# A recurrent-scan and gated-unit kernel: weight halves on two DMA queues, powers on GpSimd, and a narrower load of one matrix

## The chip, the cores and the metric

The kernel runs on one core of a Trainium2 chip (trn2). The metric is device time in microseconds (us), and I quote the median of the runs. A run whose time lies more than 1.5% above the fastest run of the same kernel is marked slow and is left out of ratios. Each profile is of a single run. Engine names are those of the profile: PE is the matmul engine TensorE, PEld its weight loads, DVE is VectorE, ACT is ScalarE, POOL is GpSimd, and SP is SyncE, which here only issues DMA transfers. A "q" after an engine's name means its instruction sequencer.

## The reference

Two branches read the same layer-normalised x (2048 tokens of 448 features). Branch A is a diagonal complex recurrence over the tokens, branch B a gated unit with 1792 hidden features.

```python
xn = layernorm(x)                                   # 2048 x 448
# A: recurrence of 448 complex states
dt      = exp(log_dt)
Lam_bar = exp(dt * (Lambda_re + 1j * Lambda_im))
Bu      = xn @ (((Lam_bar - 1) / Lam)[:, None] * (B_re + 1j * B_im)).T
h[t]    = Lam_bar * h[t-1] + Bu[t]
s       = 2 * real(h @ (C_re + 1j * C_im).T) + xn * Dskip
# B: gated unit
g       = silu((sigmoid(xn @ w_gate) * (xn @ w_up)) @ w_down)
out     = x + s * g
```

## The kernel before

The tokens are handled in four chunks of 512. For each chunk PE does the gate and up products (into `gu`, from where ScalarE and DVE take them out again into `hF`; this I call an eviction), the B product (xn with B_re and B_im, transposed to `bT`), the down product and the output product. DVE runs the scan (a hardware scan along the tokens) and the rotations around it. Once chunk 0 has reached the scan, PE and DVE are both full until near the end, so what can be gained lies in the head, before that point.

The order of the instructions on each engine is not the order of the text. A list scheduler inside the kernel (the planner, below) gives each operation an assumed cost, and sorts. `add("SP", 1.2, ...)` puts an operation that is assumed to take 1.2 us on SyncE. `chain=True` keeps the order of the text for DMA issues on one engine. A change of an assumed cost or of a transfer can reorder other engines too.

These are the parts that the change touches.

```python
def tload(keys, o, i, nbytes, r=(), chain=True):     # a transposing DMA, issued by SyncE
    add("SP", 1.2, lambda: Q.dma_start_transpose(out=o, in_=i), r=r, w=keys,
        dma=nbytes * 1.5, chain=chain)

# loads in the head: two queues, SyncE ("SP") and ScalarE ("ACT")
BLK = {"g": [(0, 2), (2, 4), (4, 7)], "u": [(0, 3), (3, 7)]}   # column blocks of w_gate, w_up
for t in range(4):
    load_x(t, 1, ("SP", "ACT")[t % 2])
load_w("SP", "g", 0, 0)                              # half 0: partitions 0-63
load_w("ACT", "g", 1, 0)                             # half 1: partitions 64-127
# ... parameters, then the other w_gate blocks ...
load("SP", "dbc", ...)                               # skip vector
load_x(4, 4)
for b in (0, 1):
    load_w("SP", "u", 0, b)                          # both halves of w_up on SyncE
    load_w("SP", "u", 1, b)

def columns():                                       # per-state parameters
    # ... PE turns three rows into columns, pv holds them ...
    add("ACT", 1.3, lambda: A.preload_act_table_set("exp_and_others"), ...)
    add("ACT", 0.2, lambda: A.activation(dt_b[:], pv[:, 0, :], ACT.Exp), ...)
    # ... four small DVE operations ...
    add("ACT", 0.2, lambda: A.activation(r_col[:], arg[:], ACT.Exp), ...)

def b_load():                                        # B, 448 x 448, to its transpose
    for i, m in enumerate((A_B_re, A_B_im)):
        tload([("bT", i)],  bT[:, 0:3, i, :], m[:, 0:384],   D * 768)
        tload([("bT3", i)], bT[:, 3:4, i, :], m[:, 320:448], D * 256)   # 128 columns
    # the last 64 states sit on partitions 64-127; copy them to 0-63 as well
    add("DVE", 0.53, lambda: V.tensor_copy(out=bT[0:H, 3, :, :], in_=bT[H:P, 3, :, :]), ...)
    for i in range(2):
        add("POOL", 0.9, lambda i=i: G.tensor_copy(out=bT6[:, :, i*H:i*H+H],
                                                   in_=bT[:, :, i, 384:448]), ...)

# issued by SyncE after b_load: eight transposes of chunk 1's xn (xnT), then w_down
```

448 is 3 x 128 + 64. Before the change the last transpose of each matrix takes 128 columns (320 to 447), of which 64 overlap the ones that were already loaded.

## Time and profile before

The median is 196.21 us (195.19 to 196.59) in three runs. The profiled run has a span of 195.0 us.

| before | us |
|---|---|
| first gate matmul | 9.15 |
| PE gaps, start to start: ScalarE's evictions late | 20.08 to 22.11 |
| PE gaps: DVE late (behind its wait for B_im) | 29.47 to 31.53 |
| PE gaps: DVE late | 34.57 to 35.74 |
| first B matmul | 34.55 |
| first scan on DVE | 40.66 |
| first gate matmul of chunk 1 | 42.77 |
| last PE instruction starts | 189.90 |

The page cuts the span into 40 slices of 4.9 us. Each digit is a busy share in tenths; PEclk is the clock that was granted to TensorE, the DMA row the mean busy share of the 16 DMA engines, and the GB/s row what they moved. The last line counts packets by size.

```profile
PE   7799696899999999999989999999999999999990
DVE  3736978999999999999999999999999999992074
PEclk9999999999999999999999999999999999999999
DMA  5899994399700014300004410000001000101002
GB/s 139 203 211 220 159 161 90 79 316 182 210 0 3 0 27 87 78 0 0 0 5 104 98 37 24 0 24 3 24 0 47 3 0 0 52 25 47 0 27 67
DMA packets 30166, 13.41 MB, mean 69 GB/s; under 512 B 19651, under 2 KB 30150, under 8 KB 30150
```

From the ninth slice on PE and DVE read 9 almost throughout, until near the end. The holes in PE (the two 6s and the 8 between them and the run of 9s) are all in the first eight slices.

The windows view gives the busy time of each engine in a stretch, in this order: stretch, its length, then PE, PEld, DVE, ACT and POOL with the number of instructions, then PEclk, DMA share and GB/s.

```profile
20.00:40.00 20.00, 15.71 (x127) 7.47 (x123) 17.86 (x38) 14.51 (x23) 10.50 (x32) 1.00 0.78 120
40.00:165.00 125.00, 122.75 (x899) 56.98 (x904) 124.69 (x205) 59.26 (x78) 16.61 (x28) 1.00 0.20 48
```

Between 20 and 40 us PE is busy 15.71 us of 20. Between 40 and 165 us DVE is busy 124.69 us of 125 and PE 122.75. Nothing can be gained there by feeding them sooner.

The waits view says which engine and line waited for what: us in total, times, longest.

```profile
DVE xd L427 <- DMA dbc<-in_A_Dskip_dram: 2.6, 1, 2.6
ACT c_r L512 <- DVE c_arg L504: 2.2, 1, 2.2
PE gu L653 <- DVE hF L670: 1.7, 1, 1.7
PE gu L653 <- ACT hF L667: 1.7, 1, 1.7
DVE bT L598 <- DMA bT<-in_A_B_im_dram: 1.6, 1, 1.6
```

The 20 us hole is a chain: DVE waited for the skip vector, so the argument `c_arg` came late, ScalarE stood at its second exponential (`c_r`), then loaded a table for 1.28 us, and the evictions `hF` that PE needed came after that. The hole at 29.5 us begins with DVE waiting for B_im before it could copy the half.

SyncE's own timeline (start, us, what it issued and how many) shows when the transposes went out:

```profile
13.06 1.36 SPq L328 DMA_DIRECT2D wU<-in_B_w_up_dram  x1
14.47 8.87 SPq L346 DMA_TRANSPOSE bT<-in_A_B_re_dram  x2
23.38 2.74 SPq L346 DMA_TRANSPOSE bT<-in_A_B_im_dram  x2
26.34 11.26 SPq L346 DMA_TRANSPOSE xnT<-xn  x8
37.65 0.59 SPq L328 DMA_DIRECT2D wd<-in_B_w_down_dram  x1
```

### The profile page before, as it was taken

What the parts mean: (1) busy time and instruction counts of PE and PEld (TensorE: products, weight loads), DVE (VectorE), ACT (ScalarE), POOL (GpSimd) and SP (SyncE); (2) the same over time, 40 slices, a digit from 0 to 9 for tenths busy, and PEclk for the clock granted to TensorE, in tenths of its full rate; (3) what the DMA queues carried; (4) which work ended last, traced back from release to release, by engine and by line L of the source; (5) the groups of instructions that cost most, each with busy time, mean ns of one, the idle gap of its engine ahead of it and who ended that gap; (6) DMA issues with size and microseconds to landing.
All of it is one profiled execution on the core that took longest, in us unless ns stands there. A gap on an engine that the chain in (4) does not pass through costs nothing.

```text
span 195.0 us, 3448 instructions
## 1 busy us (share of the span) xinstructions
PE 181.0 (93%) x1334; PEld 87.8 (45%) x1341; DVE 170.6 (87%) x313; ACT 85.7 (44%) x120; POOL 31.4 (16%) x85
## 2 busy tenths in 40 slices
PE   7799696899999999999989999999999999999990
PEld 2475353344445444444435444444435444455560
DVE  3736978999999999999999999999999999992074
ACT  2525996274877735324566341253336161211110
POOL 3220847100000770000257100000000000000000
PEclk9999999999999999999999999999999999999999
DMA  5899994399700014300004410000001000101002
GB/s 139 203 211 220 159 161 90 79 316 182 210 0 3 0 27 87 78 0 0 0 5 104 98 37 24 0 24 3 24 0 47 3 0 0 52 25 47 0 27 67
DMA packets 30166, 13.41 MB, mean 69 GB/s; under 512 B 19651, under 2 KB 30150, under 8 KB 30150
## 3 DMA queue, kind: packets, MB, share of 16 engines
q1 hardware_dynamic: 28930, 12.51, 29.9%
q10 hardware_dynamic: 1220, 0.69, 1.4%
q8 instruction: 10, 0.16, 0.4%
q14 instruction: 6, 0.05, 0.1%
HBM read 6.77 MB, written 1.84 MB: 44 GB/s over the span
## 4 chain that ended last, share of the span: by engine, by line
DVE 55%; PE 21%; SPq 9%; issue 7%; DMA 5%; ACT 1%; DVEq 0%
DVE hF L670 12%; DVE wv L759 9%; PE gu L653 5%; PE gu L820 5%; SPq L346 5%; PE acc L845 4%; PE acc L820 4%; SPq L328 4%; DVE ta L752 3%; DVE z L755 3%; DVE tb L753 3%; DVE o_t L851 3%; DVE tb L774 3%; DMA wG<-in_B_w_gate_dram 3%; DMA bT<-in_A_B_im_dram 2%
## 5 line engine op out<-in xcount | busy, mean ns | idle before, releaser
L653 PE MATMUL gu<-xnT,wG 64*128 64x512 bf16 (+1 forms) x217 | 47.0, 359 | 2.2 <-ACT hF L667 1.7
L653 PE MATMUL gu<-xnT,wU 64*128 64x512 bf16 x196 | 46.2, 376 | 1.7 <-DVE hF L670 1.7
L654 PE MATMUL gu<-xnT,wG 64*128 64x512 bf16 (+1 forms) x217 | 47.0, 359 | 0.0
L654 PE MATMUL gu<-xnT,wU 64*128 64x512 bf16 x196 | 46.2, 376 | 0.0
L667 ACT ACTIVATE sig<-gu 128x1024 f32<-128x1024 f32 x21 | 21.5, 1023 | 36.5 <-PE gu L654 36.3
L820 PE MATMUL acc<-wd,hF 128*128 128x448 bf16 x168 | 33.8, 353 | 0.0
L820 PEld LDWEIGHTS <-hF 128*128 128x128 bf16 x224 | 21.5, 98 | 21.3 <-issue 2.1
L653 PEld LDWEIGHTS <-wG 64*128 64x128 bf16 x217 | 20.1, 95 | 22.3 <-issue 2.7
L653 PEld LDWEIGHTS <-wU 64*128 64x128 bf16 x196 | 18.0, 94 | 22.9 <-issue 2.1
L670 DVE SCALAR_TENSOR_TENSOR hF<-sig,gu 128x1024 bf16<-128x1024 f32 x21 | 25.3, 1207 | 0.0
L759 DVE TENSOR_TENSOR_SCAN wv<-c_r,st,z 128x512 bf16<-128x512 f32 x18 | 23.0, 1277 | 0.0
L845 PE MATMUL acc<-cT,hT 128*128 128x448 bf16 x105 | 21.8, 353 | 0.0
L654 PEld LDWEIGHTS <-wG 64*128 64x128 bf16 x217 | 19.9, 95 | 2.5 <-issue 2.5
L654 PEld LDWEIGHTS <-wU 64*128 64x128 bf16 x196 | 17.9, 94 | 2.1 <-issue 2.0
L716 ACT CAST bus<-gu 128x1024 bf16<-128x1024 f32 x12 | 12.0, 1010 | 14.7 <-PE gu L705 14.7
L851 DVE TENSOR_TENSOR o_t<-acc,xd 128x448 bf16<-128x448 f32 x15 | 9.2, 613 | 9.2 <-PE acc L845 9.2
L705 PE MATMUL gu<-xnT,bT 128*128 128x512 bf16 x65 | 15.3, 379 | 1.1 <-issue 1.1
L845 PEld LDWEIGHTS <-hT 128*128 128x128 bf16 x119 | 11.5, 98 | 10.1 <-issue 0.4
L826 ACT ACTIVATE g_t<-acc 128x448 bf16<-128x448 f32 x12 | 6.4, 537 | 18.3 <-PE acc L820 18.3
L403 POOL TENSOR_SCALAR veb<-mv 128x2 bf16<-128x2 bf16 x6 | 2.7, 449 | 56.4 <-DVE mv L390 56.2
L389 DVE BATCH_NORM_STATS2 bst<-x_all 128x6 f32<-128x448 bf16 x16 | 9.4, 614 | 2.5 <-DMA x_all<-in_A_x_dram 2.5
L820 PE MATMUL gu<-wd,hF 128*128 128x448 bf16 x56 | 10.8, 352 | 0.0
(128 smaller groups left out, 242.2 us busy)
## 6 DMA issues: line engine op xcount, KB each, us to landing
out_dram<-o_t SPq DMA_DIRECT2D x15, 112.0 KB, 1.7
wd<-in_B_w_down_dram SPq DMA_DIRECT2D x1, 1568.0 KB, 7.1
x_all<-in_A_x_dram SPq DMA_DIRECT2D x3, 448.0 KB, 4.3
wU<-in_B_w_up_dram SPq DMA_DIRECT2D x2, 448.0 KB, 11.1
wG<-in_B_w_gate_dram SPq DMA_DIRECT2D x2, 336.0 KB, 4.5
wU<-in_B_w_up_dram SPq DMA_DIRECT2D x2, 336.0 KB, 9.8
wG<-in_B_w_gate_dram SPq DMA_DIRECT2D x2, 224.0 KB, 5.3
wG<-in_B_w_gate_dram ACTq DMA_DIRECT2D x2, 224.0 KB, 5.0
```

Source lines behind the costliest of these rows:

```text
L346: add("SP", 1.2, lambda: Q.dma_start_transpose(out=o, in_=i), r=r, w=keys, dma=nbytes * 1.5, chain=chain)
L389: add("DVE", 0.53, lambda: V.bn_stats(out=bst[b][:], in_=x_all[:, t, :]), r=[("x", t)], w=[("bst", b)])
L653: T.matmul(gu[a][:, 0, ts], lhsT=w_[0:H, s, ms], rhs=x[0:H, s, ts], start=(s == 0), stop=(s == 6))
L654: T.matmul(gu[a][:, 1, ts], lhsT=w_[H:P, (s + 1) % 7, ms], rhs=x[H:P, s, ts], start=(s == 0), stop=(s == 6))
L667: add("ACT", act(1024), lambda: A.activation(th, gu[a][:], ACT.Tanh, scale=0.5), r=[("gu", a)], w=[tk])
L670: add("DVE", dve1(1024), lambda: V.scalar_tensor_tensor(out=ho, in0=th, scalar=1.0, in1=gu[a][:], op0=ALU.add, op1=ALU.mult), r=[("gu", a) ...
L705: T.matmul(gu[a][:, i, :], lhsT=bT[:, kt, i, pt * P:pt * P + P], rhs=x[:, 2 * kt, :], start=False, stop=(kt == 2))
L716: add("ACT", act(1024), lambda u=u, a=a: A.copy(out=bus[u][:], in_=gu[a][:]), r=[("gu", a)], w=[("bus", u)])
L759: dve(1.194, lambda k=k: V.tensor_tensor_scan(out=wv[:, k, :], data0=rb, data1=z[:, k, :], initial=(st[pt][:, k, :] if c else 0.0), op0=AL ...
L820: T.matmul(d, lhsT=hF[c % 2][:, m, h, js], rhs=wd[:, ft, :], start=(ft == 0), stop=(ft == FT - 1))
L845: T.matmul(y, lhsT=hT[c % 2][:, hm, js], rhs=cT[:, cm, c0:c1], start=(i == 0), stop=(i == 6))
L851: add("DVE", dve1(n), lambda od=od, y=y, c0=c0, c1=c1: V.tensor_tensor(out=od, in0=y, in1=xq[:, c0:c1], op=ALU.add), r=[key, ("xd", q)], w ...
```

## The change

The intent is a shorter head. The two halves of each weight matrix arrive side by side on two queues, in fewer and larger blocks. The exponentials of the parameters become powers of e on GpSimd, which saves ScalarE a table load and takes small operations from DVE. Parameters and x tiles 4 to 7 are issued by GpSimd. The first transposes on PE lose a helper copy, tile 1's eviction is split between ScalarE and DVE, and w_down is issued before chunk 1's transposes. For B_re the last transpose takes just the 64 columns that are needed, straight to partitions 0 to 63, so that DVE's half copy can go. The scheduler's model of DMA times changes as well.

```diff
-    BLK = {"g": [(0, 2), (2, 4), (4, 7)], "u": [(0, 3), (3, 7)]}
+    BLK = {"g": [(0, 2), (2, 7)], "u": [(0, 7)]}
 ...
+    for k in range(3):
+        load_p("POOL", k)
     load_w("SP", "g", 0, 0)
     load_w("ACT", "g", 1, 0)
+    load_w("ACT", "g", 1, 1)
+    load_w("ACT", "u", 1, 0)
     load_w("SP", "g", 0, 1)
+    load_w("SP", "u", 0, 0)
     load("SP", "dbc", ...)
-    (both halves of w_up, and x tiles 4-7, on SyncE)
 ... columns():
-        add("ACT", 1.3, lambda: A.preload_act_table_set("exp_and_others"), ...)
-        add("ACT", 0.2, lambda: A.activation(dt_b[:], pv[:, 0, :], ACT.Exp), ...)
+        small(tt(dt_b[:], eb, pv[:, 0, :], ALU.pow), ["pv", "expc"], ["dt"])    # GpSimd
 ...
-        add("ACT", 0.2, lambda: A.activation(r_col[:], arg[:], ACT.Exp), ...)
+        small(tt(r_col[:], eb, arg[:], ALU.pow), ["arg", "expc"], ["r"])        # GpSimd
 ... b_load():
             tload([("bT", i)], bT[:, 0:3, i, :], m[:, 0:384], D * 768)
-            tload([("bT3", i)], bT[:, 3:4, i, :], m[:, 320:448], D * 256)
-        add("DVE", 0.53, lambda: V.tensor_copy(out=bT[0:H, 3, :, :], in_=bT[H:P, 3, :, :]), ...)
+            if i:
+                tload([("bT3", i)], bT[:, 3:4, i, :], m[:, 320:448], D * 256)
+            else:
+                tload([("bT3", i)], bT[0:H, 3:4, i, :], m[:, 384:448], D * 128)
 ... (the bT6 copies on GpSimd are split to match)
+    load_x(4, 4, "POOL", r=[("w", "g", 1, 6)])
     b_load()
+    load("SP", "wd", ...)                                   # moved ahead of chunk 1
 ... (warm-up matmuls, the wrap copy of xn and its transpose, the scheduler's DMA model: cut)
```

More of the change, by code (lines that the diff above doesn't have):

```diff
@@ L69 @@
 class Op:
-    __slots__ = ("idx", "eng", "cost", "fn", "pre", "suc", "late", "start", "end", "dma", "lat", "name", "left")
+    __slots__ = ("idx", "eng", "cost", "fn", "pre", "suc", "late", "start", "end", "dma", "lat", "name", "left", "rate")
 class Plan:
@@ L80, in __init__, with add @@
         self.last_of = {}
-    def add(self, eng, cost, fn, r=(), w=(), dma=0, lat=None, chain=False, name=""):
+    def add(self, eng, cost, fn, r=(), w=(), dma=0, lat=None, chain=False, name="", rate=230e3):
         o = Op()
@@ L85, in add @@
         o.lat = LAT.get(eng, 0.0) if lat is None else lat
-        o.pre, o.suc = {}, []
+        o.pre, o.suc, o.rate = {}, [], rate
         o.start = o.end = None
@@ L189, in solve @@
         dma_free = {}
+        landed = []
         while todo:
@@ L205, in solve @@
                 if e == "POOL":
-                    o.lat = 8.0
+                    o.lat = 6.0
                 else:
-                    q = dma_free[0] = max(dma_free.get(0, 0.0), o.end + 1.0) + o.dma / 280e3
-                    o.lat = q + 0.6 - o.end
+                    k = len(landed)
+                    if k >= 8:
+                        o.end = free[e] = max(o.end, landed[k - 8] + o.cost)
+                    q = dma_free[e] = max(dma_free.get(e, 0.0), o.end + 1.2) + o.dma / o.rate
+                    o.lat = q + 0.8 - o.end
+                    landed.append(q + 0.6)
             todo -= 1
@@ L302 @@
     veb = sbt("veb", [NT, 1])
-    halfc, negc = sbt("halfc", [1], FP32), sbt("negc", [1], FP32)
+    halfc, negc, expc = (sbt(n, [1], FP32) for n in ("halfc", "negc", "expc"))
     sdb = sbt("sdb", [NT, 1])
@@ L323, with load @@
     tag = lambda *k: k
-    def load(eng, key, nbytes, o, i, cost=0.45, r=()):
+    def load(eng, key, nbytes, o, i, cost=0.45, r=(), rate=230e3):
         e = {"SP": Q, "ACT": A, "POOL": G}[eng]
-        add(eng, 0.12 if eng == "ACT" else cost, lambda: e.dma_start(out=o, in_=i), w=[key] if not isinstance(key, list) else key,
-            r=r, dma=nbytes, chain=True)
+        add(eng, cost, lambda: e.dma_start(out=o, in_=i), w=[key] if not isinstance(key, list) else key,
+            r=r, dma=nbytes, chain=True, rate=rate)
     def load_x(t0, n, q="SP", r=()):
@@ L342, in load_w @@
              wgt[k][ps, :, m0 * P:m1 * P],
-             wsrc[k][:, c0 + m0 * P:c0 + m1 * P].rearrange("(s p) f -> p s f", p=H), r=r)
+             wsrc[k][:, c0 + m0 * P:c0 + m1 * P].rearrange("(s p) f -> p s f", p=H), cost=0.65, r=r, rate=145e3)
     def tload(keys, o, i, nbytes, r=(), chain=True):
@@ L354 @@
     add("POOL", 0.1, lambda: G.memset(negc[:], -1.0), r=["consts"], w=["consts"])
+    add("POOL", 0.1, lambda: G.memset(expc[:], math.e), w=["expc"])
     add("POOL", 0.1, lambda: G.memset(epsc[:], EPS), w=["epsc"])
@@ L362, with load_p @@
     add("ACT", 0.05, lambda: A.preload_act_table_set("sqrt_and_others"), w=["sqrttab"], lat=1.5, chain=True)
-    for t in range(4):
-        load_x(t, 1, ("SP", "ACT")[t % 2])
+    def load_p(eng, k):
+        load(eng, ("vrow", k), D * 2, vrow[k:k + 1, :], (A_log_dt, A_Lambda_im, A_Lambda_re)[k].unsqueeze(0), cost=0.25)
+    load_x(0, 1, "SP")
+    load_x(1, 1, "ACT")
+    load_x(2, 1, "SP")
+    load_x(3, 1, "ACT")
+    for k in range(3):
+        load_p("POOL", k)
     load_w("SP", "g", 0, 0)
     load_w("ACT", "g", 1, 0)
-    for k, vec in enumerate((A_log_dt, A_Lambda_im, A_Lambda_re)):
-        load("ACT" if k < 2 else "SP", ("vrow", k), D * 2, vrow[k:k + 1, :], vec.unsqueeze(0), cost=0.25)
+    load_w("ACT", "g", 1, 1)
+    load_w("ACT", "u", 1, 0)
     load_w("SP", "g", 0, 1)
-    load_w("ACT", "g", 1, 1)
-    for h in range(2):
-        load_w("SP", "g", h, 2)
+    load_w("SP", "u", 0, 0)
     load("SP", "dbc", P * D * 2, dbc[:], A_Dskip.unsqueeze(0).to_broadcast((P, D)))
-    load_x(4, 4)
-    for b in (0, 1):
-        load_w("SP", "u", 0, b)
-        load_w("SP", "u", 1, b)
     def warm_mm(n):
@@ L383, in f @@
                 T.matmul(gu[2][:, 0, :], lhsT=warm[:, 0:P], rhs=warm[:], start=True, stop=True)
-        add("PE", (0.43 if n > 1 else 0.22) * n, f, r=["warm"], w=[("gu", 2)])
+        add("PE", (0.38 if n > 2 else 0.22) * n, f, r=["warm"], w=[("gu", 2)])
     def stats(t):
@@ L415, in norm @@
                 r=[("x", t), ("mf", t), ("rs", t)], w=[("xn", b)])
-            add("POOL", 0.19, lambda: G.tensor_copy(out=xn[b][:, 448:512], in_=xn[b][:, 0:64]),
-                r=[("xn", b)], w=[("xnw", b)])
         else:
@@ L442, in pe_transpose, with f @@
         tp = flat(acc[a][:].bitcast(BF16)[:, 0:7 * P], 7, P)
-        def f(s0, s1):
-            for s in range(s0, s1):
+        def f():
+            for s in range(6):
                 T.transpose(tp[:, s, :], xn[b][:, s * H:s * H + P], ident[:, :])
-        add("PE", 0.36, lambda: f(0, 6), r=[("xn", b), "ident"], w=[("acc", a)])
-        add("PE", 0.06, lambda: f(6, 7), r=[("xnw", b), ("xn", b), "ident", ("acc", a)], w=[("acc", a)])
-        if t == 0:
-            add("ACT", 0.476, lambda: A.copy(out=xnT[0][:, 0:4, js], in_=tp[:, 0:4, :]),
+            T.transpose(tp[0:H, 6, :], xn[b][:, 384:448], ident[:, :])
+            T.transpose(tp[H:P, 6, :], xn[b][:, 0:H], ident[:, :])
+        add("PE", 0.46, f, r=[("xn", b), "ident"], w=[("acc", a)])
+        if t < 2:
+            add("ACT", 0.5, lambda: A.copy(out=xnT[0][:, 0:4, js], in_=tp[:, 0:4, :]),
                 r=[("acc", a)], w=[("xnT", 0, t, "a")])
@@ L453, in pe_transpose @@
                 r=[("acc", a)], w=[("xnT", 0, t, "b")])
-        elif t > 1:
+        else:
             add("DVE", 0.53, lambda: V.tensor_copy(out=xnT[0][:, :, js], in_=tp[:, :, :]),
-                r=[("acc", a)], w=[("xnT", 0, t, "a"), ("xnT", 0, t, "b")])
-        else:
-            add("ACT", 0.9, lambda: A.copy(out=xnT[0][:, :, js], in_=tp[:, :, :]),
                 r=[("acc", a)], w=[("xnT", 0, t, "a"), ("xnT", 0, t, "b")])
@@ L494, in columns @@
         pv = sbt("pv", [3, 4], FP32)
+        dt_b = C("dt", 4, BF16)
         add("DVE", 0.1, lambda: V.tensor_copy(out=pv[:].rearrange("p k i -> p i k"), in_=vps[:]), r=[("acc", a)], w=["pv"])
         dt_b = C("dt", 4, BF16)
-        add("ACT", 1.3, lambda: A.preload_act_table_set("exp_and_others"), r=[("sd", t) for t in range(4)], w=["exptab"])
-        add("ACT", 0.2, lambda: A.activation(dt_b[:], pv[:, 0, :], ACT.Exp), r=["pv", "exptab"], w=["dt"])
         lim, lre = pv[:, 1, :], pv[:, 2, :]
         K.update(lre=lre, lim=lim)
+        eb = expc[:].to_broadcast((P, 4))
         def small(fn, r, w):
-            add("DVE", 0.1, fn, r=r, w=w)
-        tt = lambda o, x, y, op: (lambda: V.tensor_tensor(out=o, in0=x, in1=y, op=op))
+            add("POOL", 0.4, fn, r=r, w=w)
+        tt = lambda o, x, y, op: (lambda: G.tensor_tensor(out=o, in0=x, in1=y, op=op))
         theta, arg, turn, r_col = C("theta"), C("arg"), C("turn"), C("r")
+        small(tt(dt_b[:], eb, pv[:, 0, :], ALU.pow), ["pv", "expc"], ["dt"])
         small(tt(theta[:], dt_b[:], lim, ALU.mult), ["dt", "pv"], ["theta"])
-        small(lambda: V.tensor_single_scalar(out=turn[:], in_=theta[:], scalar=1.0 / TWO_PI, op=ALU.mult),
+        small(lambda: G.tensor_single_scalar(out=turn[:], in_=theta[:], scalar=1.0 / TWO_PI, op=ALU.mult),
              ["theta"], ["turn"])
-        small(lambda: V.tensor_single_scalar(out=turn[H:P, 3:4], in_=theta[H:P, 3:4], scalar=-1.0 / TWO_PI,
+        small(lambda: G.tensor_single_scalar(out=turn[H:P, 3:4], in_=theta[H:P, 3:4], scalar=-1.0 / TWO_PI,
                                             op=ALU.mult), ["theta", "turn"], ["turn"])
         small(tt(arg[:], dt_b[:], lre, ALU.mult), ["dt", "pv"], ["arg"])
-        add("ACT", 0.2, lambda: A.activation(r_col[:], arg[:], ACT.Exp), r=["arg"], w=["r"])
+        small(tt(r_col[:], eb, arg[:], ALU.pow), ["arg", "expc"], ["r"])
     K = {}
@@ L517, in tables @@
         turn = C("turn")
-        add("ACT", 1.3, lambda: A.preload_act_table_set("silu_and_others"), r=["r", "dt", ], w=["silutab"])
+        add("ACT", 1.3, lambda: A.preload_act_table_set("silu_and_others"), r=[("sd", t) for t in range(4)], w=["silutab"])
         for pt in range(4):
@@ L596, in b_load @@
             tload([("bT", i)], bT[:, 0:3, i, :], m[:, 0:384], D * 768)
-            tload([("bT3", i)], bT[:, 3:4, i, :], m[:, 320:448], D * 256)
-        add("DVE", 0.53, lambda: V.tensor_copy(out=bT[0:H, 3, :, :], in_=bT[H:P, 3, :, :]),
-            r=[("bT3", 0), ("bT3", 1)], w=["bT3l"])
-        for i in range(2):
-            add("POOL", 0.9, lambda i=i: G.tensor_copy(out=bT6[:, :, i * H:i * H + H], in_=bT[:, :, i, 384:448]),
-                r=[("bT", i), ("bT3", i), "bT3l"], w=[("bT6", i)])
+            if i:
+                tload([("bT3", i)], bT[:, 3:4, i, :], m[:, 320:448], D * 256)
+            else:
+                tload([("bT3", i)], bT[0:H, 3:4, i, :], m[:, 384:448], D * 128)
+            add("POOL", 0.7, lambda i=i: G.tensor_copy(out=bT6[:, 0:3, i * H:i * H + H], in_=bT[:, 0:3, i, 384:448]),
+                r=[("bT", i)], w=[("bT6", i)])
+            hs = slice(i * H, i * H + H)
+            for h in range(2):
+                add("POOL", 0.25, lambda i=i, h=h, hs=hs: G.tensor_copy(out=bT6[h * H:h * H + H, 3, i * H:i * H + H],
+                                                                        in_=bT[hs, 3, i, 384:448]),
+                    r=[("bT3", i)], w=[("bT6", i, h)])
     def c_load():
@@ L685, in b_units @@
         slots = [next_gu() for _ in pts]
-        bk = [("bT", 0), ("bT", 1), ("bT3", 0), ("bT3", 1), "bT3l"] + ([("bT6", 0), ("bT6", 1)] if 3 in pts else [])
+        bk = [("bT", 0), ("bT", 1), ("bT3", 0), ("bT3", 1)] + (
+            [("bT6", 0), ("bT6", 1)] + [("bT6", i, h) for i in range(2) for h in range(2)] if 3 in pts else [])
         def pairs():
@@ L866, in whole @@
         ssm_pair(c, 2)
-    warm_mm(9)
+    warm_mm(11)
     for t in range(4):
@@ L876 @@
     pe_transpose(0)
-    warm_mm(1)
     pe_transpose(1)
-    warm_mm(1)
+    warm_mm(2)
     gu_mm(0, "g", 0, slots0[0], 0, 2, True)
@@ L888 @@
         gu_evac(0, "g", m, slots0[m])
+    load_x(4, 4, "POOL", r=[("w", "g", 1, 6)])
     b_load()
+    load("SP", "wd", F * D * 2, wd[:], B_w_down.rearrange("(ft p) d -> p ft d", p=P))
     def stats_for(c):
@@ L901 @@
     coeffs()
-    load("SP", "wd", F * D * 2, wd[:], B_w_down.rearrange("(ft p) d -> p ft d", p=P))
     c_load()
```

## The prediction

> **What bounds it now.** By the windows view PE is busy 98-99% from 40 us to 180 us and DVE about 100% from 40 to 165 us; the page gives PE 181.0 and DVE 170.6 of 195.0 us. So only the head (0 to 40 us) has slack. There PE stands still, by its timeline: 20.3-22.1 us (three tanh evictions wait on ScalarE, which waits at the exponential of the parameters and then loads a table, 1.28 us; DVE's argument for it sat behind a 2.6 us wait for the skip vector and the x statistics), 29.7-31.5 us (DVE waits 1.6 us for the transposed B_im, the 0.39 us half copy), and about 1 us at 34.7 (DVE backlog). The first weight matmul starts at 9.15 us, after a 0.91 us ScalarE copy of tile 1. Weight loads ran at 203-223 GB/s; one queue carried wU one half after the other, landing 19.3-24.2 us.
>
> **What changes.**
> 1. Halves on two queues at once: I estimate all weights landed by 16-17 us. Few waits were on them, so alone it buys little; it frees SyncE for B.
> 2. Powers on GpSimd (0.7-1.0 us each in this trace) replace two exponentials, one 1.28 us table load and the ScalarE stall: PE gains about 1.8 us. DVE loses some 1.1 us of small operations and the half copy.
> 3. Earlier start: no wrap copy in the transpose chain, tile 1's copy split, statistics ahead of fewer ScalarE issues: about 0.9 us.
> 4. x tiles 4-7 from GpSimd: off DVE's critical path.
> 5. w_down goes ahead of chunk 1's eight transposes on SyncE (1.25 us each): these move later.
> If all worked, PE and DVE would reach the scan stage 4-5 us sooner: 191-192 us.
>
> **The catch.** B_re's last transpose takes only 64 columns. In the built order it is no transpose but a plain copy of 64x448 single elements. The Trainium skill ("DMA: Bandwidth & Descriptors", DMA Transpose, Constraints) says an input with fewer than 128 free elements can fall back to a rearranged pattern, and its rules say a non-contiguous last dimension gives one descriptor per element; nothing before shows such a copy. That is 28,672 descriptors, 1,792 per engine. Packet medians in the trace (384 B 22 ns, 512 B 27, 896 B 41) extrapolate to about 8 ns for 2 bytes: 13-14 us as a floor; at twice that, 27 us. B_im, w_down and the chunk 1 transposes stand behind it on SyncE. Estimate: B_re flows at 16-17 us, elements to 31-40 us, B_im lands 35-43 us where PE wants it at 31; then chunk 1's transposes end near 45-54 us where PE wants them at 42. That eats the gain of 4-5 us, and with the slower rate 5-15 us more. DVE cannot make it up, being saturated afterwards.
>
> **Predicted:** 199.5 us, range 190.0 to 217.0; faster by over 2%: 0.30, within 2%: 0.26, slower by over 2%: 0.44.
>
> **What would show it.** Right: tens of thousands of 2-byte packets; the B_re copy landing over 12 us after its issue; SyncE blocked near it; PE waiting before the first B matmuls (L705 there before) or before chunk 1's gate matmuls; no exponential table load; PE's 20-22 us hole gone; first weight matmul near 8.2 us. Wrong: the element copy done in under 7 us, B matmuls at 31-32 us, DVE's first scan near 35 us instead of 40.7: then 191-192 us.
>
> **What would make it wrong.** The per-element rate, which no record here measures: much faster gives the full gain, much slower (over 20 ns) gives 215 us or more. Also DVE stalls behind the skip vector's load, or a reshuffled DVE order later.

## The result, and the profile after

The changed kernel takes 227.33 us (226.40 to 227.89, four runs) beside 196.07 us for the kernel before (195.19 to 196.59, four runs: the three above and one more). The ratio is 1.1595, with a 95% interval of 1.1534 to 1.1656. A ratio is the mean time of one kernel's fast runs over that of the other's fast runs of the same rounds, so it is not quite the ratio of the medians quoted. The change makes the kernel 16% slower, and the time lies outside the predicted range.

The page of the changed kernel, whose slices are 5.6 us long:

```profile
PE   7969950000187999999999989999999999999991
DVE  4767991000009799999999999999999999997054
PEclk9999996555569999999999999999999999999998
DMA  6999999999995850003300014200000000011001
GB/s 175 235 351 59 2 6 2 2 2 1 87 328 116 158 172 0 3 0 82 67 17 0 3 42 105 61 20 0 23 0 20 19 25 0 0 45 57 6 20 61
DMA packets 56208, 13.35 MB, mean 59 GB/s; under 512 B 47888, under 2 KB 56096, under 8 KB 56192
```

Read the DMA and GB/s rows together. In slices 5 to 10 the DMA engines are marked 90% busy or more, yet they move 1 to 6 GB/s. There are 26,042 more packets than before, for slightly fewer bytes. From the seventh slice to the tenth PE reads 0 and DVE 1 or 0, and PEclk falls to 5. Here busy engines that move almost nothing go together with very small packets.

The waits of the changed kernel, same columns as before:

```profile
POOL bT L609 <- DMA bT<-in_A_B_re_dram: 34.2, 1, 34.2
DVE ta L762 <- ACT bus L726: 32.7, 1, 32.7
PE gu L702 <- DMA bT<-in_A_B_re_dram: 29.5, 1, 29.5
```

A single wait of PE, 29.5 us long, for B_re. DVE's wait of 32.7 us comes from that one: it waits for ScalarE's copy of the B product.

SyncE's timeline after:

```profile
8.04 6.42 SPq L351 DMA_TRANSPOSE bT<-in_A_B_re_dram  x1
14.51 0.60 SPq L351 DMA_DIRECT2D bT<-in_A_B_re_dram  x1
15.16 44.05 SPq L351 DMA_TRANSPOSE bT<-in_A_B_im_dram  x2
59.25 0.58 SPq L333 DMA_DIRECT2D wd<-in_B_w_down_dram  x1
```

The call in the source is a transpose, but the second line says `DMA_DIRECT2D`: it was built as a plain copy. Its issue took 0.60 us, and the next transpose's issue then held SyncE until 57.90 us. That issue was not waiting for its completion semaphore, whose last transfer had landed at 6.92 us; it ended as the last packets of the copy did. The trace's DMA records show why: 28,672 packets of 2 bytes (64 x 448, one for each element) run from 19.97 to 57.79 us, which is 37.8 us. With 16 DMA engines sharing them, that is 37.8 us x 16 / 28,672 = 21.1 ns an element on each engine. One packet's own duration was 36.0 ns on average, so packets overlapped on an engine. The copy landed at 60.95 us, 46.4 us after its issue began, and B_im landed at 62.03 and 62.46 us. The DMA view has the copy with its size and its time from issue to landing:

```profile
bT<-in_A_B_re_dram SPq DMA_DIRECT2D x1, 56.0 KB, 46.4
```

For comparison, SyncE's timeline in the repaired kernel (the run fix_b below), where the same transfer is a transpose again:

```profile
7.94 11.09 SPq L351 DMA_TRANSPOSE bT<-in_A_B_re_dram  x2
19.07 2.74 SPq L351 DMA_TRANSPOSE bT<-in_A_B_im_dram  x2
23.76 11.43 SPq L351 DMA_TRANSPOSE xnT<-xn  x8
```

The chain that ended last, followed back (start, us, what), has this piece in the stall:

```profile
14.51 0.60 SPq L351
15.11 0.04 issue
15.16 46.87 DMA bT<-in_A_B_im_dram
```

The chain names B_im and not B_re. The first of B_im's transposes landed 1.1 us after the copy, and the chain follows whichever was needed last, so the name at that place is not the cause. One has to look at what stands ahead of it in the queue.

The windows of the changed kernel:

```profile
31.30:61.00 29.70, 0.19 (x2) 0.01 (x1) 3.33 (x10) 0.00 (x0) 0.00 (x0) 0.57 1.62 9
61.00:73.60 12.60, 10.13 (x50) 3.63 (x52) 6.23 (x8) 4.68 (x6) 4.79 (x24) 0.80 0.88 220
```

In the stall ScalarE and GpSimd are still and PE all but (0.19 us), and DVE has 3.33 us of work left in 29.7 us. The clock record is at 1.0 until 35.4 us, 0.5 until 66.1 us, then 1.0. So the first 5.1 us after the stall ran at half clock. The Trainium skill, in "TensorE: Matmul & The Clock Gate" (Part 1, the HAM clock gate), says that the clock halves after at least one idle window of about 3.4 us and returns after at least one busy window of about 3.4 us. Here it halved about 4 us after PE stopped and returned after 5.1 us, which agrees.

Point by point along the head (us; "repaired" is the run fix_b below, the changed kernel with B loaded as before):

| | before | changed | repaired |
|---|---|---|---|
| first gate matmul | 9.15 | 7.84 | 7.91 |
| first B matmul | 34.55 | 61.00 | 30.62 |
| first scan | 40.66 | 69.35 | 35.77 |
| first gate matmul of chunk 1 | 42.77 | 72.36 | 37.85 |
| last PE instruction starts | 189.90 | 220.09 | 184.57 |
| span | 195.0 | 225.2 | 189.6 |

The loss of 30.2 us in span is made as follows. PE reached the end of its work before the B product 3.4 us earlier than before (31.11 against 34.55), then stood 29.89 us, so the first B matmul came 26.45 us later. From there to chunk 1 it took 11.36 us in place of 8.22: a 1.51 us wait for B_im, the half clock, and a wait of 1.1 us for chunk 1's transposes, which were also behind (their issue had in turn waited 3.2 us for GpSimd, which had itself stood 34.2 us for the copied columns). That gives 29.6 us at the start of chunk 1. From chunk 1 to the last PE instruction the times are 147.1 us before, 147.7 changed and 146.7 repaired, so practically the whole loss had been made by 72 us.

### The profile page after: what moved, and what is told of

It reads as the page before. It is cut to its first block, busy times and chain, and to the rows that moved or that the text cites. A ratio compares the mean times of both kernels' runs of the same rounds, so it can differ in the third digit from the quotient of the medians.

```text
span 225.2 us, 3464 instructions
## 1 busy us (share of the span) xinstructions
PE 183.7 (82%) x1347; PEld 86.9 (39%) x1347; DVE 169.9 (75%) x309; ACT 83.8 (37%) x117; POOL 37.0 (16%) x96
## 4 chain that ended last, share of the span: by engine, by line
DVE 39%; DMA 25%; PE 19%; issue 7%; SPq 6%; POOL 3%; ACT 1%; DVEq 0%; POOLq 0%
DMA bT<-in_A_B_im_dram 21%; DVE hF L679 8%; PE gu L662 6%; DVE wv L769 6%; SPq L351 5%; PE gu L830 5%; PE acc L855 4%; PE acc L830 4%; DMA wG<-in_B_w_gate_dram 3%; DVE o_t L861 3%; DVE tb L784 2%; DVE ta L762 2%; DVE tb L763 2%; DVE z L765 2%; DVE ta L783 2%
## 5 line engine op out<-in xcount | busy, mean ns | idle before, releaser
L662 PE MATMUL gu<-xnT,wG 64*128 64x512 bf16 (+1 forms) x217 | 46.4, 356 | 3.6 <-DMA wG<-in_B_w_gate_dram 1.9
L663 PE MATMUL gu<-xnT,wG 64*128 64x512 bf16 (+1 forms) x217 | 46.5, 356 | 0.0
L762 DVE TENSOR_TENSOR ta<-bus,cosT 128x1024 bf16<-128x1024 bf16 x12 | 8.2, 682 | 32.7 <-ACT bus L726 32.7
L662 PEld LDWEIGHTS <-wG 64*128 64x128 bf16 x217 | 19.7, 94 | 26.0 <-issue 4.5
L702 PE MATMUL gu<-xnT,bT 64*128 64x512 bf16 x12 | 4.5, 415 | 29.5 <-DMA bT<-in_A_B_re_dram 29.5
L663 PEld LDWEIGHTS <-wG 64*128 64x128 bf16 x217 | 19.6, 94 | 0.0
L715 PE MATMUL gu<-xnT,bT 128*128 128x512 bf16 x72 | 18.2, 402 | 0.0
L702 PEld LDWEIGHTS <-bT 64*128 64x128 bf16 x12 | 1.1, 95 | 31.5 <-DMA bT<-in_A_B_re_dram 30.0
```

Of the source, the lines that this page charges most:

```text
L662: T.matmul(gu[a][:, 0, ts], lhsT=w_[0:H, s, ms], rhs=x[0:H, s, ts], start=(s == 0), stop=(s == 6))
L663: T.matmul(gu[a][:, 1, ts], lhsT=w_[H:P, (s + 1) % 7, ms], rhs=x[H:P, s, ts], start=(s == 0), stop=(s == 6))
L715: T.matmul(gu[a][:, i, :], lhsT=bT[:, kt, i, pt * P:pt * P + P], rhs=x[:, 2 * kt, :], start=False, stop=(kt == 2))
L762: dve(dve2(1024), lambda: V.tensor_tensor(out=ta[:], in0=b, in1=cosb, op=ALU.mult), [("bus", u)] + tk, [("ta", ia)])
```

## The experiments

Theory A: the single degraded transfer is the whole loss, through its own time and through everything behind it. Rival B: other parts of the change (merged weight blocks, w_down ahead of chunk 1, the powers on GpSimd, the reordered engines) bear a good part. Within A it is open why 28,672 elements take 38 us, and whether the harm is the data, the queue, or the DMA engines.

### swap_one: one instruction changed

One argument pair differs, so that the transfer is a real 128-column transpose again. The data on partitions 0 to 63 is wrong (other columns of B_re). The error is small enough to stay within the tolerance of the correctness test, but this is no usable kernel. The traces have the same order of instructions on every engine as in the changed kernel.

```diff
-                tload([("bT3", i)], bT[0:H, 3:4, i, :], m[:, 384:448], D * 128)
+                tload([("bT3", i)], bT[:, 3:4, i, :], m[:, 320:448], D * 128)
```

> The changed kernel with one instruction swapped: B_re's last transpose reads 128 columns again, so it is a real transpose (the lower half of that tile then holds the wrong columns: the result is wrong on purpose). All other instructions of all engines and their order are the same. Theory A (the element-by-element copy, and what stands behind it on SyncE, is the whole loss): 190 to 194 us, first B matmuls at 31 to 33 us. Rival B (much of the loss is the new order on SyncE, with w_down ahead of the transposes of chunk 1, or the parameters and powers on GpSimd): over 200 us.

Measured: 194.17 us (193.81 to 194.36), ratio 0.9903 (0.9854 to 0.9951). Its packets:

```profile
DMA packets 28000, 13.41 MB, mean 70 GB/s; under 512 B 19680, under 2 KB 27888, under 8 KB 27984
```

One instruction accounts for 33 us (227.33 against 194.17). The time is 0.17 us above the range I gave for Theory A, the first B matmul (32.38 us) is inside its range, and Rival B falls for the loss. The run is 2.4 us slower than the repaired kernel below; in its profile the first gate matmul waited for w_gate until 9.53 us and the clock was at half from 9.4 to 12.8 us, which the profile of fix_b does not show. The half clock is not the whole difference: one swap_one run had a mean clock of 1.000 and still took 193.81 us. The two kernels also differ in the order that the planner gave DVE. The 2.4 us stay open.

### fix_b: the change with B loaded as before

```diff
-            if i:
-                tload([("bT3", i)], bT[:, 3:4, i, :], m[:, 320:448], D * 256)
-            else:
-                tload([("bT3", i)], bT[0:H, 3:4, i, :], m[:, 384:448], D * 128)
-            (split bT6 copies)
+            tload([("bT3", i)], bT[:, 3:4, i, :], m[:, 320:448], D * 256)
+        add("DVE", 0.53, lambda: V.tensor_copy(out=bT[0:H, 3, :, :], in_=bT[H:P, 3, :, :]), ...)
+        (bT6 copies as before)
```

> The changed kernel with the B loading of before (both 128-column transposes, half copy on VectorE): a right result. Theory A: 191 to 195 us, faster than before by 1 to 2.5%, because the other parts of the change work; it should be within 1.5 us of swap_one. Rival B: over 200 us. Rival C (the other parts are worth nothing): 196 us.

Measured: 191.75 us (191.35 to 195.14, of which one run was slow), ratio 0.9775 (0.9716 to 0.9833), correct. It is faster than the kernel before, but whether by 2% is unclear, and I had expected it within 1.5 us of swap_one, which it missed (2.4 us). B_im landed at 23.4 and 23.9 us, w_down at 29.5, the last of chunk 1's transposes at 36.3. So the rest of the change is worth about what had been hoped, with DVE's half copy still in; what the half copy alone costs was not tested. Repeated as **fix_b_again**, with the same code:

> fix_b once more, on another chip: 191 to 193 us and 2 to 2.5% under before if the first measurement holds; 194 us if that one was lucky, as the near twin swap_one suggests.

It gave 193.20 us (191.98 to 194.16, six fast runs), ratio 0.9838 (0.9796 to 0.9881). The two ratios differ by 0.6%, but their intervals overlap and the chips differ, so the difference is not shown; see fix_warm0 for one thing that varies between runs.

### before_elem: the kernel before with only the new B loading

The new `b_load` is put into the kernel before; nothing else changes in the source. The scheduler moved a handful of DVE instructions for it.

> The kernel before with only the new B loading (the 64-column copy element by element). Theory A: slower by 25 to 35 us, that is 221 to 231 us, 2-byte packets for about 38 us. Rival B (the other parts cause the loss): within 3 us of before.

Measured: one fast run at 230.81 us, and three marked slow (234.76 to 235.93), so there is no ratio. Even the fast run is 34.7 us above the kernel before (196.11 in these rounds). The 2-byte packets run from 24.17 to 62.76 us (38.6 us), and the wait is the same one:

```profile
PE gu L698 <- DMA bT<-in_A_B_re_dram: 31.5, 1, 31.5
```

The degraded transfer is enough by itself. The loss is at the upper edge of what I expected, or over it. In the profiled run, a slow one, the copy begins 4 us later than in the changed kernel, and PE has a hole of 3.9 us at 18.6 us where the kernel before had one of 2.0; what makes three runs of four slow was not tested.

### half_elem: half as many elements

```diff
-                tload([("bT3", i)], bT[0:H, 3:4, i, :], m[:, 384:448], D * 128)
+                (tload([("bT3", i)],  bT[0:H, 3:4, i, 0:224],   m[0:224, 384:448],   D * 64),
+                 tload([("bT3x", i)], bT[:, 3:4, i, 224:448],   m[224:448, 320:448], D * 64))
```

Here too some of the data is wrong (the same shift as in swap_one, for half of the rows).

> The changed kernel with the element copy cut to half of its elements (rows 0 to 223; the other rows come by a 128-column transpose and are wrong on purpose). If the time goes with the number of elements at the 21 ns per element and DMA engine of the changed kernel, its packets last 19 us instead of 38 us and the run takes 208 to 210 us. If a fixed cost of such a copy dominates, it stays above 218 us.

Measured: 207.86 us (206.38 and 209.34), ratio 1.0603 (1.0486 to 1.0721). The 14,336 packets took 16.8 us, which is 18.8 ns an element on each engine, and the first B matmul came at 40.4 us. Between 14,336 and 28,672 elements that matmul moves from 40.4 to 61.0 us: 20.6 us for 896 more elements an engine, or 23 ns each. The loss goes with the count of elements.

### elem_two_queues: the elements split over two queues

Columns 384 to 415 stay on SyncE, and 416 to 447 are written as an explicit element copy on ScalarE's queue. The result is correct.

```diff
-                tload([("bT3", i)], bT[0:H, 3:4, i, :], m[:, 384:448], D * 128)
+                tload([("bT3", i)], bT[0:32, 3:4, i, :], m[:, 384:416], D * 64)
+    add("ACT", 0.65, lambda: A.dma_start(out=bT[32:64, 3, 0, :].unsqueeze(2),
+            in_=A_B_re[:, 416:448].rearrange("r c -> c r").unsqueeze(2)), w=[("bT3x", 0)], ...)
```

> The changed kernel with its element copy cut in two by partitions, 14,336 elements on SyncE's queue at the old place and 14,336 on ScalarE's behind its last weight load; the result stays right. If each queue makes or takes its elements at its own rate (21 ns per element and engine), both halves run side by side and are down near 40 us: 206 to 210 us, as half_elem. If the DMA engines themselves spend 21 ns on each element, it takes as long as one queue: landing near 60 us and 226 to 230 us.

Measured: 226.55 us (226.18 and 226.92), ratio 1.1543 (1.1475 to 1.1611). The queues of the page (packets, MB, share of 16 engines) show that the split took place:

```profile
q1 hardware_dynamic: 39952, 10.82, 39.1%
q10 hardware_dynamic: 16032, 1.86, 17.4%
```

The 2-byte packets still took 40.3 us in all (22.5 ns an element on each engine), although both queues had them in flight together from 20.4 to 52.6 us. So one queue's own rate is not the limit. The Trainium skill says, in "DMA: Bandwidth & Descriptors" (Rules for kernel authors), that spreading transfers over issuing engines does not help bandwidth since they all run on the same 16 DMA engines; this run agrees.

### fix_unread_sp and fix_unread_act: the same copy, into a tile that nobody reads

Both start from fix_b and add the element copy of B_re's last 64 columns into a scratch tile. In the first it stands at the same place in SyncE's queue, in the second it is issued by ScalarE behind the weights.

```diff
+    scr = sbt("scr", [D])
# fix_unread_sp, in b_load after B_re:
+            if i == 0:
+                tload(["scr"], scr[0:H, :].unsqueeze(1), m[:, 384:448], D * 128)
# fix_unread_act, after the last weight load:
+    add("ACT", 0.65, lambda: A.dma_start(out=scr[0:H, :].unsqueeze(2),
+            in_=A_B_re[:, 384:448].rearrange("r c -> c r").unsqueeze(2)), w=["scr"], ...)
```

> fix_b plus the element copy at its old place in SyncE's order, into a tile that nobody reads: nobody waits for its data. If the loss came only from TensorE's wait for these 64 rows, the time stays at 191 to 194 us. If what stands behind the copy in SyncE's queue (B_im, w_down, the chunk 1 transposes) carries the loss as well, the time is 221 to 229 us as with the changed kernel.

> fix_b plus the same unread element copy, issued by ScalarE behind its last weight load. Nobody waits for it and nothing stands behind it on that queue. If the loss is a matter of the order within one queue, 191 to 197 us, the other transfers a little later. If the 28,672 elements hold the shared DMA engines whatever the queue, the transposes of B and of chunk 1 come far later and the time is over 205 us.

fix_unread_sp took 228.71 us in its fast run and 232.47 in a slow one, and the profile is of the slow one. B_im landed at 64.2 us, and DVE waited for it:

```profile
DVE bT L605 <- DMA bT<-in_A_B_im_dram: 40.0, 1, 40.0
```

Nobody reads the copied data, and the loss is still there. So the harm is in what stands behind the copy in the queue.

fix_unread_act took 227.69 us in its fast run and 232.90 in a slow one, again the profiled one. The time fits the second expectation (over 205 us), but not by the way that was argued. The transfers of SyncE's queue did get through while the elements ran: B landed between 23.7 and 30.6 us (20.8 to 23.9 in fix_b), w_down at 37.6 (29.5). They and the elements did slow each other: the elements took 51.0 us here (28.5 ns each on an engine), and chunk 1's first three transposes landed at 40.3 to 45.3 us (30.1 to 32.7 in fix_b). The large loss came after that, when SyncE itself stood still. Its waits:

```profile
SPq L352 <- DMA scr<-in_A_B_re_dram: 34.0, 1, 34.0
```

Nothing of chunk 1 depends on `scr`. The trace shows eight completion semaphores used in turn by the DMA transfers of SyncE and ScalarE together. The fourth transpose of chunk 1 came to the one that the element copy still held, and it had to wait until that copy was complete (it landed at 69.89 us). PE then waited 30.6 us for chunk 1's `xnT`. A slow transfer on another queue blocked this one through a shared semaphore.

### fix_wd_late, fix_blk3, fix_act_exp: the other parts of the change

All three start from fix_b. The first puts w_down back behind chunk 1's transposes, the second uses three blocks of w_gate again, and the third puts the exponentials back on ScalarE with their table load.

```diff
# fix_wd_late
-    load("SP", "wd", ...)          # after b_load
+    load("SP", "wd", ...)          # after coeffs, as before
# fix_blk3
-    BLK = {"g": [(0, 2), (2, 7)], "u": [(0, 7)]}
+    BLK = {"g": [(0, 2), (2, 4), (4, 7)], "u": [(0, 7)]}
# fix_act_exp: columns() as in the kernel before, silu table after r and dt
```

> fix_b with w_down behind the transposes of chunk 1 on SyncE, as before. In fix_b these transposes land by 36.3 us and chunk 1 begins at 37.8 us, w_down is not needed before about 53 us. So w_down's place costs nothing: within 1 us of fix_b. If the early w_down is a gain or a loss of its own, over 1.5 us apart.

> fix_b with the gate weights in three blocks (0-2, 2-4, 4-7) on each queue in place of two (0-2, 2-7). In fix_b the third gate group waits 1.3 us at 11.1 us for the large block. Expected: that hole goes, 190.0 to 191.8 us, 0 to 1.5 us faster than fix_b. If another landing takes its place, no change.

> fix_b with the two exponentials and their table load back on ScalarE and the small operations back on VectorE. By the reading of before, the tanh evictions stall again and TensorE stands still near 20 us: 193 to 196 us, 1.5 to 3 us slower than fix_b. If the powers on GpSimd are worth nothing, 191 to 192 us.

fix_wd_late: 192.30 us (191.62 to 196.38, one slow), ratio 0.9783 (0.9743 to 0.9823), fix_b_again 0.9838; the intervals overlap. No effect of w_down's earlier place is shown.

fix_blk3: 194.27 us (193.78 to 195.17), ratio 0.9912 (0.9856 to 0.9968). The hole at 11 us is gone, as expected, but with one more transfer in the queue the lower half of w_up met a semaphore still in use, was issued at 7.28 in place of 3.27 us and landed at 21.24 in place of 19.45. Holes in PE at 27.6 and 32.0 us followed. No gain.

fix_act_exp: 194.26 us (193.93 to 194.97), ratio 0.9908 (0.9864 to 0.9952). It is slower than fix_b (0.9775) by 1.4% and than fix_b_again by 0.7%. It was run at another time. Its profile has a gap at 31.5 us (DVE late) but none at 20 us. The planner also changed the order of about 34 DVE instructions. So the powers on GpSimd may be worth between 1 and 2.5 us (194.26 against 193.20 and 191.75), but the hole at 20 us in the kernel before needed more than the exponentials: there, DVE also stood 2.6 us for the skip vector. This one is not settled.

### fix_old_loads: the loads of the kernel before, in fix_b

> fix_b with the loads of before: wU halves one after the other on SyncE, parameters from SyncE and ScalarE, x tiles 4 to 7 from SyncE. Then wU lands at 19 to 24 us and B_im near 28 us again; with TensorE at the first wU group near 21 us it waits for wU. Expected 193 to 196 us, 2 to 4 us slower than fix_b. If the new loads are worth nothing, 191 to 192.5 us.

Measured: 204.40 us (203.19 to 206.33, one slow), ratio 1.0404 (1.0352 to 1.0456), much slower than expected and slower than the kernel before with the very same loads. PE has gaps of 2.2 us at 23.7 (ScalarE late), 3.8 at 31.7 (for the half copy, which DVE, busy until then, reached only at 35.03) and 4.1 at 48.9 (DVE late), and the clock is at half from 36.6 to 40.0 and from 53.7 to 57.1 us. The kernel's scheduler, with its new DMA model, chose another order for these loads. So the run does not measure the loads alone. What it shows is that the order and the loads belong together; the value of the loads by themselves stays open.

### fix_warm, fix_warm0, fix_wd_late_warm0: the hole at 11 us and the clock

In fix_b_again PE stands from 11.25 to 12.91 us, since the merged block of w_gate lands late, and the clock drops to half after it. The remedy is to give PE dummy matmuls there. fix_warm adds them with a planned cost; the other two add 2 and 6 of them with a planned cost of zero, so that the scheduler leaves the other engines as they were.

```diff
# fix_warm
-    warm_mm(2)
+    warm_mm(5)
     ... columns()
+    warm_mm(6)
# fix_warm0 (and fix_wd_late_warm0, which starts from fix_wd_late)
     warm_mm(2)
+    warm_free(2)                    # add("PE", 0.0, ...)
     ... columns()
+    warm_free(6)
```

> fix_b with 3 more dummy matmuls before the first gate group and 6 before the third, where TensorE otherwise stands still for weights. In two profiles of like kernels (fix_b_again, swap_one) the granted clock fell to a half for 3.4 us after such a hole, in fix_b it did not, and that one was 2 us faster. If the half clock makes the spread, the clock stays at 1.0 from 7 us on and the time is 191 to 192 us in all runs. If not, 193 to 194 us as before, or more by the dummies' time.

> fix_b with 2 dummy matmuls before the first gate group and 6 before the third, entered with no cost in the planner, so that the order on VectorE, ScalarE, GpSimd and SyncE stays exactly that of fix_b (fix_warm had 132 rows of VectorE's order changed, and says nothing of the clock). If the half clock after the wait for weights makes the spread from 191.4 to 194 us: the clock is 1.0 from 7 us on and the median is 191 to 192 us. If not: 193 us or more.

> fix_wd_late with the same dummies at no planned cost. By the clock theory 191 to 192 us, and within 0.7 us of fix_warm0; if not, 192.3 us as fix_wd_late or more.

fix_warm: 195.70 us (195.24 to 197.61), ratio 1.0007 (0.9946 to 1.0068). The clock stayed at 1.0, but the planned cost changed the order on DVE (at least 64 of its 310 instructions stand elsewhere), and new gaps stand at 15.9, 32.4 and 46.0 us. It says nothing of the clock.

fix_warm0: 191.83 us (191.72 to 194.82, one slow), ratio 0.9773 (0.9749 to 0.9797). The orders on DVE, ACT, POOL and SP are identical to fix_b's. fix_wd_late_warm0: 191.83 us (191.73 to 192.37), ratio 0.9784 (0.9758 to 0.9811), so again no effect of w_down's place is seen. The windows of fix_b_again and then of fix_warm0 over the hole, with columns as above:

```profile
10.00:12.90 2.90, 1.43 (x23) 0.92 (x19) 1.05 (x3) 0.00 (x0) 0.83 (x1) 1.00 1.07 313
12.90:16.40 3.50, 3.48 (x34) 2.46 (x36) 2.56 (x6) 0.28 (x1) 3.08 (x7) 0.51 1.05 334
```

```profile
10.00:12.90 2.90, 2.90 (x33) 1.55 (x31) 1.03 (x3) 0.00 (x0) 0.84 (x1) 1.00 1.06 337
12.90:16.40 3.50, 3.50 (x62) 2.89 (x60) 2.57 (x6) 1.91 (x3) 3.08 (x7) 1.00 1.06 334
...
20.00:40.00 20.00, 20.00 (x168) 8.85 (x166) 19.06 (x33) 13.97 (x24) 12.09 (x31) 1.00 0.93 183
```

PE is busy 3.5 us in both in the second stretch, but starts 62 instructions at clock 1.00 and 34 at 0.51. The last line is the head of this kernel: from 20 to 40 us PE is busy throughout, as it already is in fix_b's profile, against 15.71 us before. Whether the drop comes differs from run to run (fix_b's own profile has a hole of 1.30 us there and no drop), which may be one reason why fix_b and fix_b_again differ. The run list agrees in part: the three fix_b_again runs with a mean clock of 0.994 or more took 191.98 to 192.85 us, the three of 0.991 or less 193.55 to 194.16. But one run of fix_warm0 took 194.82 us at a mean clock of 0.999, so the half clock is not the whole of the spread. fix_warm0 is the fastest version whose interval lies clear of 2%, and it beats both kernels. That it beats fix_b itself is not shown: 0.9773 and 0.9775 are the same. It was run at another time.

### best and best_warm: an attempt at more

Three blocks of w_gate, as in fix_blk3, with x tiles 2 and 3 in one transfer, so that the number of transfers stays the same; best_warm adds dummy matmuls with a planned cost.

```diff
-    load_x(2, 1, "SP")
-    load_x(3, 1, "ACT")
+    load_x(2, 2, "SP")
```

> fix_b with three gate blocks as in fix_blk3, and x tiles 2 and 3 in one transfer, so that the eighth transfer no longer makes the lower wU half wait for the first gate block (issue at 7.3 us in fix_blk3, 3.3 us in fix_b). Expected: wU at 19.5 us in place of 21.2, no hole at 11 us: 190 to 192 us. If the weights' bandwidth alone sets these landings, 193 to 194.5 us as fix_blk3.

> best with 2 more dummy matmuls before the first gate group and 3 before the third. If the half clock is what remains: 190 to 191.5 us. If best has no hole left, the same as best, or up to 1 us more.

Both failed: 200.93 us (200.69 to 202.19), ratio 1.0258 (1.0219 to 1.0297), and 203.11 us (199.97 to 204.93, two slow), ratio 1.0246 (1.0179 to 1.0313). ScalarE's timeline in best:

```profile
6.89 0.63 ACTq L333 DMA_DIRECT2D wU<-in_B_w_up_dram  x1
7.63 0.48 ACT L406 ACTIVATE sdb<-mv,epsc 128x1 bf16<-128x1 bf16 x2 [5.63 <-DMA wG<-in_B_w_gate_dram]
```

ScalarE's last weight issue waited for a semaphore that an earlier w_gate transfer still held, and ScalarE's square roots (`sdb`) for the normalisation stood behind it for 5.63 us. The first gate matmul came at 11.19 us in place of 7.9. That is 3.3 us of some 9 us lost against fix_b; PE has another hole of 4.9 us at 28.9 us, behind DVE, whose cause was not followed up.

## Why the prediction was wrong

**The step that failed** is the term for the element copy: "Packet medians in the trace (384 B 22 ns, 512 B 27, 896 B 41) extrapolate to about 8 ns for 2 bytes: 13-14 us as a floor; at twice that, 27 us." It measured 21.1 ns an element and 37.8 us. A straight line through packets of 384 to 896 bytes did not hold for single elements: their packets lasted 36.0 ns on average, between those of 512 and of 896 bytes, and as they overlapped, the cost of an element was 21.1 ns. The few bytes alone do not make it: the same trace has 1,569 packets of 4 bytes that lasted 9.3 ns on average (what they carry was not looked up). No record of the kernel before had such a packet in it, which the prediction said itself; the right answer to that was a much higher upper end. It did list "much slower (over 20 ns) gives 215 us or more" among what would make it wrong, and that is what came.

**Consequences of that term.** "B_im lands 35-43 us": it landed at 62 us. The sum was short as well: 16 to 17 us and the 27 us of the upper case give 43 to 44 us for the last element, where the prediction wrote 40; it came at 57.8. "with the slower rate 5-15 us more": it was 31 us more than the kernel before (227.33 against 196.07). The prediction also had the elements flow from 16-17 us; they began at 19.97 us, behind the weights. The half clock after the stall (35.4 to 66.1 us) was not foreseen. It is in the profile of each of the six kernels with the element copy.

**What was right.**
- The bound: PE and DVE are full from 40 us on, and the loss is carried unchanged to the end (147.1 us against 147.7 from chunk 1 to the last PE instruction).
- The catch itself: the call was built as a plain copy, 28,672 packets, SyncE blocked near it, and B_im, w_down and chunk 1 behind it. The Trainium skill's statement that an input below 128 free elements can fall back, and that a non-contiguous last dimension gives a descriptor for each element ("DMA: Bandwidth & Descriptors", DMA Transpose, Constraints, and Rules for kernel authors), is what this trace shows: 64 x 448 packets of 2 bytes.
- "If all worked ... 191-192 us": fix_b measured 191.75 and 193.20 us, fix_warm0 191.83.
- The first gate matmul was predicted near 8.2 us and came at 7.84. The 20 to 22 us hole is gone, and there is no exponential table load.

**What was wrong in a small way.** Weights were to be landed by 16 to 17 us; they landed at 17.9 us. "Few waits were on them" held for the kernel before, but merging w_gate's blocks made a new wait: PE stood from 11.07 to 13.15 us for blocks 2 to 6. The fear that w_down ahead of chunk 1 would delay it did not show (fix_wd_late). The powers on GpSimd as the one reason for the hole at 20 us are not shown (fix_act_exp).

**What stays open:** why an element costs 21 ns (reading single elements from memory, writing them, or something else), why swap_one is 2.4 us slower than fix_b, the value of the new loads apart from the order that the scheduler made for them, and the share of the powers on GpSimd.

## What to carry to other kernels

Look at which instruction a DMA call was built into and count its descriptors, not its bytes: here 56 KB cost 38 us, and the cure was to transpose 128 columns where 64 were needed. Here the slow transfer harmed all that stood behind it in its queue and, through completion semaphores that are used in turn, transfers on another queue (fix_unread_act); in best, the wait for such a semaphore held up even the compute instructions of ScalarE, which issues DMA. When a kernel plans its own order, compare variants whose order on the other engines is the same, or the experiment measures the planner.

## What the Trainium skill lacked or had wrong

- "DMA: Bandwidth & Descriptors" (DMA Transpose, Constraints; Rules for kernel authors) says that the fallback exists and that it makes one descriptor for each element, but gives no time for an element of it. Here it is 21.1 ns on each of 16 engines (37.8 us for 28,672), 18.8 ns with half as many, 22.5 ns over two queues, and 28.5 ns beside other transfers (fix_unread_act). The page speaks of inputs in DRAM "smaller than one xbar tile"; it would help to say that a 448 x 64 slice of a larger matrix counts as such.
- The same page (Rules) and "VectorE: DVE Perf Modes" (The three transpose paths) give a factor of 19 between a plain rearranged copy and the hardware transpose, the second page for a large innermost step of the destination; in the copy written out in elem_two_queues it is the source that is read in large steps. Here the element copy of 64 columns took 46.4 us from issue to landing, and the repaired kernel's 128-column transpose of B_im 3.3 us: a factor of 14 for half the columns, both including the wait for their turn.
- No page that I read names the wait for a reused completion semaphore as a cost. Here it held SyncE for 34.0 us (fix_unread_act), and in best ScalarE stood idle for 5.63 us behind an issue that waited in this way. "DMA: Bandwidth & Descriptors" (Rules) only advises a semaphore of its own for a DMA.
- "TensorE: Matmul & The Clock Gate" (Part 1) ties the halved clock to at least one idle window of about 3.4 us. In fix_b_again the clock was at half from 13.0 to 16.4 us after a hole of only 1.66 us (11.25 to 12.91), with PE busy 1.43 us of the 2.90 us before 12.90; a hole of 2.08 us in the changed kernel had no such effect. No run here shows what decides it.
